# A fused attention and gating kernel: order of small steps, banks of PSUM, and where attention's two parts are added

## The chip, the cores and the metric

The kernel runs on one core of a Trainium2 chip. The metric is device time in microseconds (us) of one execution. The engines are PE (matmul, with its weight loads listed as PEld), DVE (vector), ACT (activation), POOL and SP, whose queue (SPq) issues nearly all DMA transfers. PE writes its results into PSUM, eight banks of 512 float32 values for each of 128 partitions; DVE and ACT read them there.

## The reference, cut to what matters

Two blocks follow each other on 2048 tokens of width 1024. Block A is attention with a memory, block B a gated network that mixes along the tokens.

```python
# block A: 32 heads of 32, 4 segments of 512 tokens
q, k, v = (layernorm(x) @ w for w in (wq, wk, wv))      # split into heads and segments
for s in range(4):
    p     = softmax(qs @ ks.T * scale + mask)           # inside the segment
    a_dot = p @ vs
    a_mem = (phi(qs) @ M) / (phi(qs) @ z + 1e-6)        # the memory of earlier segments
    o     = g * a_mem + (1 - g) * a_dot                 # g = sigmoid(beta), for each head
    M, z  = M + phi(ks).T @ vs, z + phi(ks).sum()
h = x + o @ wo
# block B
zz = gelu(layernorm(h) @ w_in)                          # 3584 columns
z1, z2 = zz[:, :1792], layernorm(zz[:, 1792:])
out = h + (z1 * (w_sp @ z2 + b_sp)) @ w_out
```

## The kernel before, in words

All operations are recorded in program order by `_Recorder.record`, which finds for each the earlier operations that it must wait for (by 32 bytes in SBUF and by whole banks in PSUM). `emit` then writes one instruction stream for each engine, so every engine works strictly in the order of the recording. Since `emit` issues everything at line 214, all rows of the profile have that line; they are told apart by the names of tiles.

**Attention.** The loop `for n in range(LAST + 1)` makes 32 rounds: segment `s = n // 8`, group of four heads `c = n % 8`. A round computes on PE the logits in three parts (`logits(n, 0..2)`, into banks 0 to 3), the projections of K and Q for the next round (`qk`), the product of probabilities and V for the round before (`pv(n - 1)`, into banks 4 and 5, the view `PVA`), the state update (`state`, in bank 5) and one or two tiles of other work (V projections, output projections `wo`), all of which take banks 6 and 7 in turn by `next_bank`. From segment 1 on, the third logits part is joined by `mem` (queries against the memory) and `mem_norm`, which divides it into the tile `tm` on DVE. `norm(n)` on DVE takes the reciprocal of the softmax sums (`rd`), multiplies `PVA` by it, in segment 0 straight into `otok`, otherwise into the tile `ta`, and later adds `ta` and `tm` into `otok`; between the two, `state_sum` copies the state update out of bank 5 (`msum` or `upd`), and POOL adds it to the memory. POOL also masks the exponentials (`affine_select` on `e`).

`bg_pop` advances layer norms of the next tokens by one step: apply, then reciprocal root on POOL, then statistics on DVE (`stats`). `piece_loads` and `piece_norms` load rows of the input and mixing weights of block B (`nb`) and take their absolute maximum on DVE (`sqz`, `sq`) or their squares on ACT; the table `pieces` says in which round. `scale_of(16)` in round 25 sums them with a small matmul into a bank taken by `next_bank`, and DVE reduces that bank into `tot`.

**Block B.** Products are formed in a seven-product scheme of sums of blocks. `z2_step` makes the second half of the first product; `jobs2`, filled by `at(x, f)`, hangs other work behind its steps, among it the last segment's output projection (`wo_tile`, each of its two 512-column halves being added to x on DVE as `hch`). From here on banks come from the list `free`, and how it rotates sets the later order `banks`. `z1_step` makes the first half; its weight sums `sz` are formed on POOL (`sz_sum`). `gate(pr, perm)` does the mixing over tokens for each half of the tokens, with banks given by `perm`: `perm[0:3]`, `perm[3:5]` and `perm[5:7]` in three roles. Its products are named by the mixing weights' sums, `t1` to `t4` and `b11` to `b22`; for the second half these sums are made on DVE by `q_sum`. In it ACT copies partial results (`copy_u`, tile `tmp_u`), DVE forms the gated result `z1x`, and `jobs` hangs other work behind each step, among it the squares `y0_norm` on ACT and `scale_w`. The output product at the end uses banks 0 to 6 by number.

Of the kernel before, what the change touches and what calls it, by code (L numbers as in the profile page):

```python
# [262 lines left out]
def bass_sequential_preLN__memory_aug_infini_attn__mixer_gmlp__prompt_kernel(  # L263
# [401 lines left out]
    def norm(n):  # L665
        s, c = divmod(n, NQ)
        ot = OTOK[s % 2][:, :, c * 128:(c + 1) * 128].rearrange("p q (i d) -> p q i d", d=32)
        dve.reciprocal(RD[:], PVA[:, :, :, 32])
        dve.tensor_tensor(RD[:], RD[:], OMG[:, c:c + 1, :].to_broadcast([128, 4, 4]), ALU.mult)
        rb = RD[:].unsqueeze(3).to_broadcast([128, 4, 4, 32])  # L670
        if s == 0:
            dve.tensor_tensor(ot, PVA[:, :, :, 0:32], rb, ALU.mult)
        else:
            dve.tensor_tensor(TA[:], PVA[:, :, :, 0:32], rb, ALU.mult)
        if n:
            state_sum(n)
        if n == 1:
            state_sum(0)
        if s > 0:
            dve.tensor_tensor(ot, TA[:], TM[n % 2][:], ALU.add)  # L680
        if c == NQ - 1:
            for tcl in range(4):
                to_T(OT, tcl, OTOK[s % 2][:, tcl, :])
# [238 lines left out]
    def sz(g, k):  # L922
        return SZ[k - 1 + (k == 4 and g % 2)][:]

    def sz_sum(g, k):
        fc = FC[g]
        a, b, op = {1: (wz_blk(1, 0, fc), wz_blk(1, 1, fc), ALU.add), 2: (sz(g, 1), wz_blk(0, 0, fc), ALU.subtract),
                    3: (wz_blk(0, 0, fc), wz_blk(1, 0, fc), ALU.subtract),
                    4: (wz_blk(0, 1, fc), sz(g, 2), ALU.subtract)}[k]
        pool.tensor_tensor(sz(g, k), a, b, op)  # L930

    def w_half(c, eng=dve):
        if eng is act:
# [36 lines left out]
                              apply_absolute_value=True)  # L970

    pieces = {}
    for i, (n, k, q) in enumerate(((6, 0, dve), (6, 1, dve), (7, 0, dve), (7, 1, dve), (8, 0, dve), (14, 1, dve),
                                   (15, 0, dve), (15, 1, dve), (16, 0, dve), (17, 1, dve), (10, 0, act), (11, 1, act),
                                   (12, 0, act), (13, 1, act), (18, 2, act), (19, 3, act))):
        pieces.setdefault(n, []).append((NB[k], SQZ, i, q))
# [15 lines left out]
    for n in range(LAST + 1):  # L992
        s, c = divmod(n, NQ)
        f1, f2, f3, f4 = [], [], [], []
        if n < LAST:
            f1, f2 = [("qk", n + 1, 1)], [("qk", n + 1, 0)]
        if s == 0:
            f3 = [("v", 0, c, 1)] if c < 4 else [("v", 1, c - 4, 0)]
        elif s < NSEG - 1:
            if c < 2:  # L1000
                f3, f4 = [("v", s, 2 * c, 1)], [("v", s, 2 * c + 1, 1)]
            elif c < 6:
                f3, f4 = [("wo", s - 1, c - 2, 0)], [("wo", s - 1, c - 2, 1)]
            else:
                f3, f4 = [("v", s + 1, 2 * (c - 6), 0)], [("v", s + 1, 2 * (c - 6) + 1, 0)]
        elif c < 2:
            f3, f4 = [("v", s, 2 * c, 1)], [("v", s, 2 * c + 1, 1)]
        elif c < 6:
            f3, f4 = [("wo", s - 1, c - 2, 0)], [("wo", s - 1, c - 2, 1)]
        elif c == 6:  # L1010
            f3, f4 = [("z2", 2, 0, 0)], [("z2", 2, 4, 1)]
        else:
            f1, f2 = [("z2", 2, 1, 2)], [("z2", 2, 5, 3)]
            f3, f4 = [("z2", 0, 0)], [("z2", 0, 4)]

        def fill(lst):
            for u in lst:
                {"v": proj_v, "wo": wo, "qk": proj_qk, "z2": z2_group, "qmm": q_part, "qout": qk_out,
                 "vmm": v_part, "vout": v_out}[u[0]](*u[1:])

        if s < NSEG - 1 and 0 <= c - 2 * (s == 0) < 4:
            t = c - 2 * (s == 0)
            ln_tasks(XCH[t], XNT[(s + 1) % 2], t)
        if s < NSEG - 2 and c >= 4:
            x_load(4 * (s + 2) + c - 4)
        if s > 0 and c == 1:
            xr_load(4 * (s - 1))

        if n == 0:
            fill([("vmm", 0, 3, 0, 7, 0, 5)])  # L1030
            f1 = [("vmm", 0, 3, 0, 7, 5, 8), ("vout", 0, 3, 0, 7)] + f1
            f2 = [("qmm", 1, 7, 0, 8), ("qout", 1, 0, 7), ("vmm", 0, 0, 1, 6, 0, 2)]
            f3 = [("vmm", 0, 0, 1, 6, 2, 8), ("vout", 0, 0, 1, 6)]
        piece_loads(n + 1, act)
        logits(n, 0)
        fill(f1)
        if n > 0:
            pv(n - 1, range(3))
        logits(n, 1)
        if n > 0:  # L1040
            pv(n - 1, (3,))
        if n != 2:
            bg_pop()
        fill(f2)
        if n == 2:
            bg_pop()
        logits(n, 2)
        if n < LAST:
            phi_exp(n + 1)
        piece_norms(n, act)  # L1050
        if n == 0:
            gates()
            mask_g()
        while n == LAST and staged:
            z2_gelu(*staged.pop(0))
        fill(f3)
        if n < LAST:
            phi_max(n + 1)
        bg_pop()
        fill(f4)  # L1060
        bg_pop()
        if n == 25:
            scale_of(16)
        piece_norms(n, dve)
        piece_loads(n + 1, dve)
        if n == 0:
            rot["n"] = 1
        if n == 1:
            sp.dma_start(WO[:], wcols(A_wo, 0, D))
        if n in (24, 26):  # L1070
            win_load(n - 24)
        if n == 24:
            pool.memset(ONES[:], 1.0)
            pool.memset(MHZ[:], -0.5)
            scale_in(SQZ, 10, 1.0)
        if n == 26:
            scale_end(1)
            w_half(0)
        if n == 28:
            w_half(2)  # L1080
        if n == 29:
            w_sum(0, 3, WS[0, 0])
            w_sum(0, 2, WS[0, 0])
        if n == 30:
            w_sum(0, 4, WS[0, 0])
            hn_sum(0, 1, 0)
            hn_sum(0, 1, 1)
            xr_load(4 * (NSEG - 1))
            win_load(1)
            win_load(3)  # L1090
        if n == LAST:
            hn_sum(0, 2, 0)
            hn_sum(0, 2, 1)
            hn_sum(0, 3, 0)
            hn_sum(0, 3, 1)
            w_sum(0, 1)
            hn_sum(0, 4, 0)
            hn_sum(0, 4, 1)
# [49 lines left out]
    def at(x, f, *a):  # L1148
        jobs2.setdefault(x, []).append((f, a))

    def wo_tile(tcl):
        for half in range(2):
            wo(NSEG - 1, tcl, half)
            wide.add(free[-1])
            bg_pop()

    def sj_load(i):
        r, h = 14 + i // 2, i % 2
# [14 lines left out]
    at(8, w_sum, 1, 2, WS[0, 1])  # L1173
    at(12, w_sum, 1, 1)
    for i in range(4):
        at(8 + 2 * i, wo_tile, i)
    for i in range(4):
        at(34 + 8 * i, sj_load, i)
        at(44 + 8 * i, sj_norm, i)
# [216 lines left out]
    def z1_step(g, k):  # L1396
# [18 lines left out]
        if k == 1:  # L1415
            if zb[g, 1] not in full:
                pe.matmul(PS[:, zb[g, 1], 448:512], IDENT[:], IDENT[:, 0:64], start=False, stop=False,
                          skip_group_check=True)
            act.activation(bank(zb[g, 1]), b, ACTF.Copy)
        elif k == 6:  # L1420
            dve.tensor_copy(u2, b)
        elif k == 5:
            act.activation(u3, b, ACTF.Copy)
            if g < 13:
                for x in (1, 2):
                    sz_sum(g + 1, x)
        elif k == 7:
            dve.tensor_tensor(u3, b, u3, ALU.add)
            late.append(lambda: z1_out(fc + 7, 2 * p + 1, u3))
            if g < 13:  # L1430
                sz_sum(g + 1, 3)
        elif k == 2:
            z1_out(fc, 2 * p, b)
            if g == 0:
                sz_sum(1, 4)
        elif k == 4:
            z1_out(fc + 7, 2 * p, b)
        else:
            dve.tensor_tensor(u2, b, u2, ALU.add)
            late.append(lambda: z1_out(fc, 2 * p + 1, u2))  # L1440
            if g < 12:
                sz_sum(g + 2, 4)
# [186 lines left out]
    q_sum("t2")  # L1629
    s_sum(3, 0)  # L1630
    q_sum("t3")

    OBG = {"b12": 0, "b22": 2, "t1": 1, "t2": 3, "t3": 4, "t4": 5}
    OBW = {"b11": 0, "b21": 1}
# [65 lines left out]
        jobs.setdefault((g, k), []).append((f, a))  # L1700

    for r in range(14):
        job(r // 7, (r % 7) // 2, y0_norm, r)
    for h in range(4):
        job(2 + (h + 1) // 4, (h + 1) % 4, y0_conv, h)
        job(3 + (h + 1) // 4, (h + 1) % 4, y_sum, h + 1, 0)
    job(2, 0, y0_scale)
    job(0, 0, q_sum, "t4")
    job(0, 0, scale_w)
    for r in range(7):  # L1710
        job(1, 0, ob_load, "b12", r)
# [14 lines left out]
        for f, a in jobs.get((g, k), ()):  # L1726
            f(*a)

    gate(1, [banks[k] for k in (0, 3, 5, 1, 2, 4, 6)], each=each1)

    def o_prod(b, a, w, first, lo=0, hi=512):
        for i in range(7):
# [3 lines left out]
    def iv(g):  # L1736
        return (INVO0 if g < 3 else INVO)[:]

    def o_p1(g):
        o_prod(g % 3, y_blk(0, 0, g), "b11", True)  # L1740
        act.activation(OT4[g % 2][0][:], bank(g % 3), ACTF.Copy, scale=iv(g))

    def o_adds(g, ks=(1, 2, 3)):
        for k in ks:
# [4 lines left out]
        dve.scalar_tensor_tensor(o, PS[:, b, lo:hi], iv(g), add, ALU.mult, ALU.add)  # L1749

    def o_p2(g):
        o_prod(g % 3, y_blk(0, 1, g), "b21", False)

    def o_c11(g):
        f = FIN2[g % 4][:, 0, 0, :]
        o_stt(g, f, g % 3, f)
        fin_out(g, 0, 0)

    fin_in(2)
# [2 lines left out]
    o_adds(0)  # L1762
    ob_sum("t4", 3)
    for g in range(NG):
        bb, bc = 3 + g % 2, 5 + g % 2
        end = g == NG - 1
        last = ((bc, 0, 512),) if not end else ((bc, 0, 384), (7, 384, 512))
        f1, f12, f22, f21 = OT4[g % 2]
# [65 lines left out]
```

## Time and profile before

| what | value |
|---|---|
| median of 3 runs | 744.46 us (743.98 to 744.66) |
| the profiled execution's own time | 744.07 us |
| its span in the profile | 742.4 us |
| PE busy | 730.3 us (98%) |
| DVE busy | 582.3 us (78%) |
| ACT busy | 478.6 us (64%) |
| POOL busy | 276.4 us (37%) |
| granted PE clock | 1.0 throughout |

The profile shows one execution. Times in the timeline count from the start of the span: attention runs to about 310 us, the second half of block B's first product to about 396, its first half to about 483, the mixing of the first half of the tokens to 568, of the second half from 582 to about 655, the output product to the end. In a timeline row the first number is the start, the second the duration of the merged run, then come the engine, the operation, the tiles (out<-in), the shape and how many instructions were merged; a bracket gives the engine's idle time before the row and what ended it. Matmul records of 512 columns last 0.38 us, though one starts every 0.22 us, because they are pipelined; single matmul records can be missing.

### The profile page before, as it was taken

To read this page: it belongs to the slowest core of one execution; us is meant where nothing else is said; L and a number is where in the kernel's file an instruction comes from. 1 tells how busy PE (TensorE), PEld (TensorE's weight loads), DVE (VectorE), ACT (ScalarE), POOL (GpSimd) and SP (SyncE) were. 2 spreads that over 40 slices of the span, in tenths; PEclk is the share of its full clock that TensorE was granted. 3 is DMA by queue.
4 is the path that set the end of the run, shared out by engine and by line. 5 is a ranking of instruction groups with operands and counts; after the bars stand their busy time and mean duration, and the time that the engine had idled before them with its cause. 6 is when DMAs were issued, how large, how long until landed. Compare 5 with 4: busy or idle time off the path is not lost.

```text
span 742.4 us, 13475 instructions
## 1 busy us (share of the span) xinstructions
PE 730.3 (98%) x5333; PEld 351.7 (47%) x5399; DVE 582.3 (78%) x1026; ACT 478.6 (64%) x684; POOL 276.4 (37%) x424
## 2 busy tenths in 40 slices
PE   8999999999999999999999999999999999999998
PEld 4444445445555445545554444444444444444444
DVE  5577889889988989878896767875556688866676
ACT  6777889888887888826886669966866283210000
POOL 2565455555654343110054899600000100005342
PEclk9999999999999999999999999999999999999999
DMA  9655668457635852645050036399539211031311
GB/s 302 173 171 125 136 145 178 130 147 167 172 100 158 255 178 58 171 125 132 29 141 1 1 57 129 54 202 183 173 119 320 81 41 35 1 114 64 107 57 57
DMA packets 148798, 92.64 MB, mean 125 GB/s; under 512 B 105984, under 2 KB 132864, under 8 KB 148224
## 3 DMA queue, kind: packets, MB, share of 16 engines
q1 hardware_dynamic: 147920, 91.00, 47.0%
q8 instruction: 42, 0.69, 0.4%
q10 hardware_dynamic: 816, 0.79, 0.3%
q14 instruction: 20, 0.16, 0.1%
HBM read 56.11 MB, written 12.58 MB: 93 GB/s over the span
## 4 chain that ended last, share of the span: by engine, by line
PE 87%; DVE 8%; ACT 2%; issue 1%; DMA 1%; POOL 0%; DVEq 0%
PE ps L214 87%; DVE stats L214 2%; DVE sqz L214 1%; DMA wv<-in_A_wv_dram 1%; DVE hch L214 1%; DVE otok L214 1%; DVE pqk L214 1%; ACT e L214 1%; DVE ta L214 0%; DVE rd L214 0%; DVE rdm L214 0%; DVE etmp L214 0%; POOL sz L214 0%; DVE tm L214 0%; DVE sq L214 0%
## 5 line engine op out<-in xcount | busy, mean ns | idle before, releaser
L214 ACT ACTIVATE e<-ps 128x2048 bf16<-128x2048 f32 (+1 forms) x96 | 152.7, 1591 | 21.3 <-PE ps L214 20.6
L214 POOL TENSOR_SCALAR_AFFINE_SELECT e<-e 128x512 bf16<-128x512 bf16 x128 | 91.2, 726 | 123.1 <-ACT e L214 122.9
L214 PE MATMUL ps<-xnT,wk 128*128 128x512 bf16 x233 | 59.6, 380 | 1.8 <-ACT v L214 0.4
L214 PE MATMUL ps<-wv,xnT 128*128 128x512 bf16 x255 | 59.3, 380 | 1.4 <-DMA wv<-in_A_wv_dram 1.0
L214 POOL TENSOR_TENSOR ot<-ot,fin 128x512 f32<-128x512 f32 x21 | 27.8, 1351 | 86.5 <-ACT ot L214 86.5
L214 PE MATMUL ps<-wo,oT 128*128 128x512 bf16 x254 | 57.9, 380 | 0.9 <-DVE hch L214 0.8
L214 PE MATMUL ps<-xnT,wq 128*128 128x512 bf16 x226 | 54.0, 379 | 1.6
L214 PEld LDWEIGHTS ps<-v,e 128*128 128x128 bf16 x1280 | 38.8, 96 | 14.0 <-issue 6.5
L214 ACT ACTIVATE ot<-ps,invo 128x512 f32<-128x512 f32 x7 | 4.8, 688 | 60.8 <-PE ps L214 60.8
L214 PE MATMUL ps<-v,e 128*128 128x33 bf16 x1280 | 42.2, 178 | 0.0
L214 POOL TENSOR_TENSOR sz<-wzh 128x512 f16<-128x512 f16 x28 | 34.0, 1217 | 11.2 <-PE ps L214 11.1
L214 DVE BATCH_NORM_STATS2 zst<-z 128x6 f32<-128x448 bf16 x64 | 38.1, 611 | 0.0
L214 ACT ACTIVATE tmp_u<-ps,invy 128x512 f32<-128x512 f32 x14 | 9.6, 686 | 44.2 <-PE ps L214 44.2
L214 PEld LDWEIGHTS ps<-wo,oT 128*128 128x128 bf16 x256 | 24.0, 98 | 28.6 <-DVE hch L214 1.3
L214 PE MATMUL ps<-z2h,sy 128*128 128x512 f16 (+2 forms) x182 | 37.4, 363 | 0.0
L214 PEld LDWEIGHTS ps<-xnT,wk 128*128 128x128 bf16 x256 | 22.6, 98 | 30.6 <-issue 4.5
L214 ACT ACTIVATE qk<-ps 128x512 bf16<-128x512 f32 x48 | 28.8, 600 | 12.9 <-PE ps L214 12.9
L214 PEld LDWEIGHTS ps<-wv,xnT 128*128 128x128 bf16 x256 | 23.2, 98 | 27.9 <-DMA wv<-in_A_wv_dram 1.2
L214 DVE TENSOR_TENSOR zt<-ps,zt 128x512 f32<-128x512 f32 x28 | 19.1, 686 | 22.1 <-PE ps L214 17.6
L214 PE MATMUL ps<-qk 32*128 32x128 bf16 (+3 forms) x512 | 34.5, 302 | 0.7 <-DVE tm L214 0.5
L214 PEld LDWEIGHTS ps<-xnT,wq 128*128 128x128 bf16 x256 | 23.5, 97 | 22.9 <-issue 0.2
L214 ACT ACTIVATE ps<-ps 128x512 f32<-128x512 f32 (+1 forms) x42 | 23.9, 568 | 14.0 <-PE ps L214 14.0
(280 smaller groups left out, 1673.3 us busy)
## 6 DMA issues: line engine op xcount, KB each, us to landing
nb<-in_B_w_in_dram SPq DMA_DIRECT2D x16, 448.0 KB, 4.0
nb<-in_B_w_sp_dram SPq DMA_DIRECT2D x14, 512.0 KB, 4.7
w_out<-in_B_w_out_dram SPq DMA_DIRECT2D x6, 896.0 KB, 5.3
xch<-in_A_x_dram SPq DMA_DIRECT2D x16, 256.0 KB, 4.3
xr<-in_A_x_dram SPq DMA_DIRECT2D x16, 256.0 KB, 3.9
out_dram<-hch SPq DMA_DIRECT2D x16, 256.0 KB, 2.4
w_spT<-stg SPq DMA_DIRECT2D x16, 256.0 KB, 4.1
out_dram<-fin SPq DMA_DIRECT2D x31, 128.0 KB, 1.7
```

What stands on the lines that cost most here:

```text
L214: ins = getattr(e, op.name)(*op.args, **op.kw)
```

## The change

It does this:

- In `norm`, segments 1 to 3 write the product of `PVA` and `rd` back into `PVA` in PSUM instead of into `ta`, and the sum with `tm` follows at once, ahead of `state_sum`'s copy.
- The absolute maximum with index 4 moves from round 8 to round 5, and its load from the end of round 7 to the end of round 4.
- In round 8 the first `bg_pop` comes after `logits(n, 2)`.
- After `scale_of(16)` the rotation of banks 6 and 7 goes on by one.
- The first output projection of the last segment is split: its second half comes one `z2_step` later.
- One weight sum, `sz_sum(1, 2)`, runs on DVE instead of POOL.
- The sum `t4` is made before the second `gate` instead of behind its first step, and the squares `y0_norm` start one step later, two for each step.
- The output product takes its banks from the second `gate`'s order (`obank`) instead of by number.

```diff
@@ norm(n)
-            dve.tensor_tensor(TA[:], PVA[:, :, :, 0:32], rb, ALU.mult)
+            dve.tensor_tensor(PVA[:, :, :, 0:32], PVA[:, :, :, 0:32], rb, ALU.mult)
+        if s > 0:
+            dve.tensor_tensor(ot, PVA[:, :, :, 0:32], TM[n % 2][:], ALU.add)
         if n:
             state_sum(n)
         if n == 1:
             state_sum(0)
-        if s > 0:
-            dve.tensor_tensor(ot, TA[:], TM[n % 2][:], ALU.add)
@@ sz_sum
-    def sz_sum(g, k):
+    def sz_sum(g, k, eng=pool):
...
-        pool.tensor_tensor(sz(g, k), a, b, op)
+        eng.tensor_tensor(sz(g, k), a, b, op)
@@ pieces
-    for i, (n, k, q) in enumerate(((6, 0, dve), (6, 1, dve), (7, 0, dve), (7, 1, dve), (8, 0, dve), (14, 1, dve),
+    for i, (n, k, q) in enumerate(((6, 0, dve), (6, 1, dve), (7, 0, dve), (7, 1, dve), (5, 0, dve), (14, 1, dve),
@@ the loop over rounds
-        if n != 2:
+        if n not in (2, NQ):
             bg_pop()
         fill(f2)
         if n == 2:
             bg_pop()
         logits(n, 2)
+        if n == NQ:
+            bg_pop()
...
         if n == 25:
             scale_of(16)
+            rot["n"] += 1
@@ the last segment's output projection
-    def wo_tile(tcl):
-        for half in range(2):
-            wo(NSEG - 1, tcl, half)
-            wide.add(free[-1])
-            bg_pop()
+    def wo_half(tcl, half):
+        wo(NSEG - 1, tcl, half)
+        wide.add(free[-1])
+        bg_pop()
...
-        at(8 + 2 * i, wo_tile, i)
+        at(8 + 2 * i, wo_half, i, 0)
+        at(8 + 2 * i + (i == 0), wo_half, i, 1)
@@ z1_step, k == 5
-                    sz_sum(g + 1, x)
+                    sz_sum(g + 1, x, dve if (g, x) == (0, 2) else pool)
@@ before the second gate
     q_sum("t3")
+    q_sum("t4")
@@ jobs of the second gate
     for r in range(14):
-        job(r // 7, (r % 7) // 2, y0_norm, r)
+        job(*divmod(1 + r // 2, 4), y0_norm, r)
...
-    job(0, 0, q_sum, "t4")
     job(0, 0, scale_w)
...
-    gate(1, [banks[k] for k in (0, 3, 5, 1, 2, 4, 6)], each=each1)
+    perm1 = [banks[k] for k in (0, 3, 5, 1, 2, 4, 6)]
+    gate(1, perm1, each=each1)
@@ output product
+    obank = [perm1[k] for k in (1, 2, 0, 4, 3, 6, 5)]
...
-        o_prod(g % 3, y_blk(0, 0, g), "b11", True)
-        act.activation(OT4[g % 2][0][:], bank(g % 3), ACTF.Copy, scale=iv(g))
+        o_prod(obank[g % 3], y_blk(0, 0, g), "b11", True)
+        act.activation(OT4[g % 2][0][:], bank(obank[g % 3]), ACTF.Copy, scale=iv(g))
...
-        bb, bc = 3 + g % 2, 5 + g % 2
+        bb, bc = obank[3 + g % 2], obank[5 + g % 2]
```

More of the change, by code (lines that the diff above doesn't have):

```diff
@@ L1751, in o_p2 @@
     def o_p2(g):
-        o_prod(g % 3, y_blk(0, 1, g), "b21", False)
+        o_prod(obank[g % 3], y_blk(0, 1, g), "b21", False)
     def o_c11(g):
         f = FIN2[g % 4][:, 0, 0, :]
-        o_stt(g, f, g % 3, f)
+        o_stt(g, f, obank[g % 3], f)
         fin_out(g, 0, 0)
```

## The prediction

> **What bounds the kernel now.** I read the page's busy times first, then the list of waits for PE, then the stretches of the timeline around each of those waits.
>
> ```profile
> PE 730.3 (98%) x5333; PEld 351.7 (47%) x5399; DVE 582.3 (78%) x1026; ACT 478.6 (64%) x684; POOL 276.4 (37%) x424
> ```
>
> PE is busy for 730.3 of 742.4 us, and no other engine is near that. The matmuls stay, so only PE's 12 us of idle time can be won, and part of those lie before the first matmul and behind the last. The list of waits names the others:
>
> ```profile
> PE ps L214 <- DVE hch L214: 1.0, 2, 0.8
> PE ps L214 <- DVE tm L214: 0.5, 1, 0.5
> PE ps L214 <- ACT tmp_u L214: 0.5, 1, 0.5
> PE ps L214 <- ACT v L214: 0.4, 1, 0.4
> ...
> PE ps L214 <- POOL sz L214: 0.3, 1, 0.3
> ```
>
> The columns are the total, the count and the longest. These are single events, and the change touches each of them. Here is each in the timeline, with what PE waited for:
>
> ```profile
> 85.33 3.63 PE L214 MATMUL ps<-wv,xnT 128*128 128x512 bf16 x16
> ...
> 86.70 1.41 DVE L214 BATCH_NORM_STATS2 stats<-xch 128x6 f32<-128x512 bf16 x2
> ...
> 88.72 0.69 DVE L214 TENSOR_TENSOR tm<-ps,rdm 128x512 f32<-128x512 f32 x1
> ...
> 89.47 0.39 PE L214 MATMUL ps<-qk 32*128 32x512 bf16 x4 [0.51 <-DVE tm L214]
> ...
> 249.78 0.17 DVE L214 TENSOR_REDUCE tot<-ps 128x1 f32<-128x16 f32 x1 [0.31 <-PE ps L214]
> ...
> 250.39 1.90 PE L214 MATMUL ps<-xnT,wk 128*128 128x512 bf16 x7 [0.35 <-ACT v L214]
> ...
> 318.00 1.90 PE L214 MATMUL ps<-wo,oT 128*128 128x512 bf16 x8 [0.78 <-DVE hch L214]
> ...
> 400.48 1.45 POOL L214 TENSOR_TENSOR sz<-wzh 128x512 f16<-128x512 f16 x1 [6.86 <-PE ps L214]
> ...
> 403.31 1.89 PE L214 MATMUL ps<-z1x,sz 128*128 128x512 f16 x8 [0.29 <-POOL sz L214]
> ...
> 594.48 1.90 PE L214 MATMUL ps<-t4g,z2h 128*128 128x512 f16 x8 [0.49 <-ACT tmp_u L214]
> ```
>
> The first row gives the rate: sixteen matmuls in 3.63 us, the last recorded for 0.38, so one starts every 0.217 us. The record of the last before a gap thus overhangs by 0.16 us, and a bracket understates what PE lost by about that.
>
> **Part by part.**
>
> *Statistics after the memory normalisation (round 8).* `bg_pop` now stands behind `logits(8, 2)`, so the two statistics (1.41 us) and their aggregate (0.21) follow `tm` instead of delaying it. Rounds 8, 9, 10 and 11 begin at 79.40, 89.47, 98.89 and 108.31: round 8 lasts 10.07 us where its followers last 9.42, and the difference of 0.65 is the prize. Afterwards `tm` ends near 87.9, 0.9 before PE wants its bank. This pop issues only statistics: no DMA, nothing on POOL.
>
> *One absolute maximum from round 8 to round 5.* Its 2.01 us on DVE now come at about 66.3 and push K's copy for round 7 from 66.45 to 68.3. That bank is wanted by V at 69.96, and `etmp` waits for ACT until 71.65 anyway. Q's copy ends near 70.9, and its reader starts at 71.79: 0.9 of cover. Its 448 KB load moves with it from SP's queue at the end of round 7, where it stood ahead of attention's transposes, to the end of round 4, ahead of an x load. The next load into that buffer must now wait for the maximum, until 68.3, where SP was free at 67.95: 0.3 us later, and its reader starts at 72.64 against 4.0 us to land. I put it at nothing; if the cover fails, the whole 0.3 to 0.9 goes on the path.
>
> *Banks after `scale_of(16)` (round 25).* K's first matmul comes 0.74 us after the logits there, against 0.33 in the rounds before and after (240.45 to 240.78, 259.25 to 259.58): 0.41 is lost to V's evacuation. K now takes the bank that `tot` reads. That reduce ends at 249.95, and DVE hands over in 0.06 (`tm` to 89.47), so K starts at 250.01 instead of 249.98. Gain 0.38.
>
> *Attention's sum from PSUM, 24 rounds.* These groups carry the price:
>
> ```profile
> L214 DVE TENSOR_TENSOR otok<-ta,tm 128x512 bf16<-128x512 f32 x24 | 22.3, 930 | 0.3
> ...
> L214 DVE TENSOR_TENSOR zt<-ps,zt 128x512 f32<-128x512 f32 x28 | 19.1, 686 | 22.1 <-PE ps L214 17.6 <-ACT z1T L214 4.4
> ...
> L214 DVE TENSOR_TENSOR ta<-ps,rd 128x512 f32<-128x512 f32 x24 | 16.6, 691 | 0.8
> ```
>
> The sum reads `ta` and `tm` from SBUF and takes 930 ns in the mean, 691 at best and over 1,000 beside POOL's selects. With one operand in PSUM its nearest row is `zt`, 686. The product keeps its inputs but writes PSUM in place; no DVE instruction of this trace writes there. ACT does, in 568 ns (`ps<-ps`) against 600 into SBUF (`qk<-ps`), so I take 691 for the product, with 0.6 below and twice the streaming time, 1.22, above, if reading and writing one bank took turns. The pair falls from 1.62 to 1.38 us, DVE loses 24 x 0.24 = 5.8 us, and nearly none of it is on the path. Two waits stand on this chain: 0.11 at 165.05, where the old sum took 0.86, and 0.31 near 269, where it already took 0.69. The first gives 0.05, the second nothing. Behind the sum, the state copy and POOL's update come up to 0.7 later; the banks are wanted again 5 us on.
>
> [...]
>
> *Halves of the last projection.* The second half waits for the first one's sum, since it takes the same bank. Lost: 0.78 + 0.16 = 0.94. Four 448-column matmuls (319.73 to 320.49, 0.76) now go in between and only change places. The rest, 0.18, stays. Gain 0.76.
>
> *One weight sum to DVE.* PE lost 0.29 + 0.16 = 0.45. POOL's first sum ends at 401.93, and its second fills 402.01 to 403.16. DVE's sum, 0.42 (`z2h<-z2h`, 512 f16), is done by 402.5; PE wants it at 402.86. DVE stands until then with `wzh` (0.74) queued behind, so that ends near 403.2; next comes `zt` at 403.12, which delays only its own activation. Gain 0.45.
>
> *Norms and `t4`.* `tmp_u` (593.75 to 594.42) was late because ACT ran two squares (0.84 and a read of 0.19 each) first. Without them it follows its matmuls, at 592.3 to 593.0, and PE wants the bank at 593.82. `t4` (2.29) moves in front of `z1x`, where DVE was idle for 4.67. ACT then runs six squares of 0.95, not five, before `tmp_u` of the next group: 593.0 to 598.7, where that can start at 599.2. Six follow in the next group instead of five, so the last ends near 611.4 instead of 610.4, still ahead of the next `tmp_u` (611.95) and of PE's sum of them (615.21). Gain 0.49 + 0.16 = 0.65.
>
> *Output banks.* They follow the new order of banks so that each first use falls on one long free. PE shows no gap at that seam, so zero; without this, about 0.75 (a `z1x` row).
>
> **Sum:** 0.65 + 0.38 + 0.05 + 0.76 + 0.45 + 0.65 = 2.94 us. The profiled execution took 744.07, so 741.13; the median of the runs, 744.46, lies 0.39 higher and would give 741.52. I take the middle, 741.3.
>
> **Rivals.**
>
> 1. *Part of it becomes other waits.* What is late next is close in two places: `tot` at 249.95 against 249.98, DVE's weight sum 0.4 ahead. If these two pay nothing, the gain is 2.1 and the time 742.2. For it: the margins; against: the rest have 0.8 or more. 0.14.
> 2. *The write into PSUM costs 1.22.* The pair is then 1.91. At 165.05 it grows from 0.69 + 0.86 = 1.55, so 0.36 comes back; near 269 DVE runs without a pause through two rounds whose pairs grow from 1.38, so 1.06. Rounds with `hch` or an absolute maximum behind the pair may add another 0.2 to 1. That leaves a gain of 0.5 to 1.3, 743.2 to 744, within 0.2%. ACT's row speaks against. 0.07.
> 3. *Slower: both operations at 1.22.* The pair of 2.45 is 0.83 longer than the mean now. An ordinary round has 0.41 of slack (`tm` ends at 98.42 and hands over in 0.06, PE starts at 98.89), so each of the 16 rounds of segments 1 and 2 pays 0.42, 6.7 in all; less 2.94 that ends near 748. It decides from a pair of about 2.2, where 16 x 0.18 eats the gain. Nothing in the rows speaks for it but that the form is new. 0.05.
> 4. *The change does not do what it says:* the new order of banks puts a wait where there was none. Each step above finds its bank read 0.1 us or more before it is wanted, except where said. A whole new wait of 0.8 to 1.5 us leaves 742.1 to 742.8. 0.05.
>
> **Chances and range.** The forecast gets 0.69. A measurement here cannot tell less than 0.2%, or 1.5 us, from no change. Faster holds the forecast, the first rival and most of the fourth: 0.87. Same 0.07, slower 0.06. The range goes from 740.7 (the runs' spread of 0.35 each way and all of the projection's wait) to 742.5 with rival 1: about 0.8.
>
> **What would show it.** In the changed profile PE's list should have lost `tm`, `tmp_u`, `sz` and `v`, with `hch` down to 0.2 or 0.4 and the 0.3 near 268 still there. `otok<-ps,tm` should stand near 690 and `ps<-ps,rd` near 690. A `ps<-ps,rd` over 0.95, a PE wait on `tm` in many rounds, or one on `qk` near 71 would prove me wrong.

## The result, and the profile after

| what | before | after |
|---|---|---|
| median of 6 runs each, taken together | 744.22 us (743.43 to 745.21) | 741.11 us (740.89 to 741.8) |
| the profiled execution's own time | 744.07 us | 741.11 us |
| its span | 742.4 us | 739.5 us |
| first round-3 logits to last matmul (below) | 697.98 us | 695.42 us |

The ratio of the times is 0.996, with a 95% interval of 0.9947 to 0.9972: faster by 0.3 to 0.5%. The forecast was 741.3. It was nearly met, but not by its own sum: one of its gains was given back, and scatter in the first microseconds of the execution filled part of the hole.

That scatter matters for all that follows. The programs of all these runs are nearly the same in the first 13 us, and yet these move by up to 2.1 us between executions. The traces with a granted clock of 1.00 throughout reach round 3 between 40.91 and 41.66 us. Two traces with a lower clock at the start come later: in that of the first experiment (e1) it was 0.87 between 5 and 10 us and 0.79 between 10 and 15, with round 3 at 43.19; in that of the last kernel (best_max_27) it was 0.73 and 0.93 (0.998 over the whole execution in both), with round 3 at 42.45. A single time can therefore not settle a term of 0.4 us. So I also compare a **stretch** of each trace: from the 512-column logits matmuls of round 3 (at 41.33 us before, 41.05 after) to the start of the last matmul, worked out from the recorded starts. Two traces of the kernel after give 695.42 and 695.45. Of the kernel before there is one trace.

First the line of PE, and PE's list of waits (total, count, longest) of the kernel after.

```profile
PE 733.4 (99%) x5399; PEld 351.7 (48%) x5399; DVE 579.5 (78%) x1027; ACT 478.0 (65%) x684; POOL 267.0 (36%) x423
```

```profile
PE ps L214 <- DVE etmp L214: 1.2, 1, 1.2
PE ps L214 <- DVE tm L214: 0.6, 1, 0.6
PE ps L214 <- DMA wv<-in_A_wv_dram: 0.6, 1, 0.6
PE ps L214 <- DVE xnT L214: 0.3, 1, 0.3
PE ps L214 <- DVE hch L214: 0.2, 1, 0.2
```

PE's busy time went up only in the records: all 5399 matmuls stand here, where the page before had 5333. The list says more. `tmp_u`, `sz` and `v` are gone, and so is the 0.8 of `hch`. `tm` is not: it stands at 0.6, and this is not the old event. `etmp`, `wv` and `xnT` belong to the start of the program. Next, the timeline of the kernel after around the seven places (start, duration, engine, operation, tiles, count, idle before and its releaser):

```profile
86.89 0.69 DVE L214 TENSOR_TENSOR tm<-ps,rdm 128x512 f32<-128x512 f32 x1
...
87.50 1.41 DVE L214 BATCH_NORM_STATS2 stats<-xch 128x6 f32<-128x512 bf16 x2
...
88.59 0.40 PE L214 MATMUL ps<-qk 32*128 32x512 bf16 x4
...
164.00 0.40 PE L214 MATMUL ps<-qk 32*128 32x512 bf16 x4
...
248.73 0.17 DVE L214 TENSOR_REDUCE tot<-ps 128x1 f32<-128x16 f32 x1 [0.31 <-PE ps L214]
...
248.96 1.90 PE L214 MATMUL ps<-xnT,wk 128*128 128x512 bf16 x8
...
267.67 0.39 PE L214 MATMUL ps<-qk 32*128 32x512 bf16 x4 [0.59 <-DVE tm L214]
268.26 1.90 PE L214 MATMUL ps<-xnT,wk 128*128 128x512 bf16 x8 [0.20 <-DVE hch L214]
...
317.04 1.90 PE L214 MATMUL ps<-wo,oT 128*128 128x512 bf16 x8
...
399.95 0.42 DVE L214 TENSOR_TENSOR sz<-sz,wzh 128x512 f16<-128x512 f16 x1 [1.40 <-POOL sz L214]
400.27 2.75 PE L214 MATMUL ps<-z1x,sz 128*128 128x512 f16 x12
...
591.64 1.89 PE L214 MATMUL ps<-t4g,z2h 128*128 128x512 f16 x8
```

The five waits of PE that the forecast shows with a bracket have none any more; the logits at 267.67 have a new one. These are the first ones of round 28, and they wait for `tm` of round 27. Matching the PE instructions of the two traces one by one gives what each place moved (minus: the kernel after comes earlier by so much more):

| place (us in the kernel after) | step, us | forecast |
|---|---|---|
| start, first 13 us | -0.29 | nothing |
| end of round 8, 88.59 | -0.58 | -0.65 |
| logits of round 17, 164.00 | -0.18 | -0.05 |
| K after `scale_of(16)`, 248.96 | -0.39 | -0.38 |
| logits of round 28, 267.67 | **+0.48** | nothing |
| second half of the projection, 317.04 | -0.76 | -0.76 |
| weight sum, within the row at 400.27 | -0.46 | -0.45 |
| `t4`, 591.64 | -0.66 | -0.65 |

Without the start the steps add up to -2.55, and the stretches differ by 2.56 (697.98 - 695.42); the forecast's sum was -2.94. With the start the steps come to -2.84, as the spans do.

The operations in the new form, from the groups by line and shape (count | busy time, mean ns | idle before); the third line is POOL's:

```profile
L214 DVE TENSOR_TENSOR ps<-ps,rd 128x512 f32<-128x512 f32 x24 | 16.8, 699 | 0.8
L214 DVE TENSOR_TENSOR otok<-ps,tm 128x512 bf16<-128x512 f32 x24 | 16.6, 692 | 0.8
L214 POOL TENSOR_SCALAR_AFFINE_SELECT e<-e 128x512 bf16<-128x512 bf16 x128 | 83.9, 669 | 127.1 <-ACT e L214 127.1
```

The product written into PSUM in place takes 699 ns, the sum 692, a pair of 1.39 us where 1.38 was forecast. The two rivals that needed 1.22 for one or both of them fall. The 1.22 was an estimate, and the rows of the kernel before bear it: DVE's copies from PSUM take 284 ns there for 132 float32 columns (`upd`) and 673 for 512 (`zt`), so 512 columns more would cost some 524, and 691 + 524 is 1.215 us.

**Where the 0.48 went.** Between `tot` and `tm`, DVE runs through two rounds of work. These are rows of the timeline of DVE in the kernel before:

```profile
249.78 0.17 DVE L214 TENSOR_REDUCE tot<-ps 128x1 f32<-128x16 f32 x1 [0.31 <-PE ps L214]
...
254.85 0.18 DVE L214 TENSOR_TENSOR rd<-rd,omg 128x16 f32<-128x16 f32 x1
...
257.03 0.17 DVE L214 TENSOR_SCALAR rdm<-ps 128x16 f32<-128x16 f32 x1 [0.55 <-ACT e L214]
...
264.36 1.13 DVE L214 TENSOR_SCALAR wih<-win,sc 128x3584 f16<-128x3584 bf16 x1
```

In the same trace POOL's masks start behind `rd` and `wih`:

```profile
255.21 2.49 POOL L214 TENSOR_SCALAR_AFFINE_SELECT e<-e 128x512 bf16<-128x512 bf16 x3 [2.40 <-ACT e L214]
...
264.40 2.18 POOL L214 TENSOR_SCALAR_AFFINE_SELECT e<-e 128x512 bf16<-128x512 bf16 x2 [2.12 <-ACT e L214]
```

And these are DVE and POOL in the kernel after:

```profile
253.78 1.22 POOL L214 TENSOR_SCALAR_AFFINE_SELECT e<-e 128x512 bf16<-128x512 bf16 x2 [2.01 <-ACT e L214]
253.80 0.63 DVE L214 TENSOR_TENSOR rd<-rd,omg 128x16 f32<-128x16 f32 x1
...
255.81 0.16 DVE L214 TENSOR_SCALAR rdm<-ps 128x16 f32<-128x16 f32 x1
...
262.96 2.07 POOL L214 TENSOR_SCALAR_AFFINE_SELECT e<-e 128x512 bf16<-128x512 bf16 x2 [2.12 <-ACT e L214]
263.13 1.41 DVE L214 TENSOR_SCALAR wih<-win,sc 128x3584 f16<-128x3584 bf16 x1
...
266.92 0.69 DVE L214 TENSOR_TENSOR tm<-ps,rdm 128x512 f32<-128x512 f32 x1
```

`tot` starts on the small matmul of `scale_of(16)`, which stands ahead of K. The rotation moves K, not `tot`, so it doesn't move DVE's run. From the start of `tot` to the hand-over of `tm`, 0.06 before the logits, DVE takes 18.78 us before (249.78 to 268.56) and 18.88 after (248.73 to 267.61). Before, 0.55 of that was idle, since `rdm` had to wait for its round; with the hand-over this pause cost 0.63 (the sum starts 1.24 before `rdm` there, 0.61 after). With PE 0.39 earlier, 0.24 of it should have stayed. But the masks on POOL came earlier too, one now 0.02 ahead of `rd` and one 0.17 ahead of `wih`. From start to start, `rd` to the product grew from 0.21 to 0.67, and `wih` to the next from 1.05 to 1.33, together by 0.74. That is the whole pause and 0.11 more, against 0.10 in the run. So nothing of the 0.39 reached round 28, and 0.09 was lost on top.

The rows show how long the two operations stood beside the masks. The first of the two masks runs for about 0.61 (half of 1.22), from 253.78 to 254.39, and `rd` ends at 254.43, 0.63 after its start; in the kernel before, where it was done before the mask began, it took 0.18. With the same 0.61 for the second mask, `wih` stood 0.44 beside it and took 0.28 longer (1.41 against 1.13), where `rd` stood 0.59 beside its mask and took 0.45 longer: each pays some 0.15 less than the overlap. How a mask slows an operation of DVE is not shown by these runs. The group of masks points the same way: 726 ns in the mean before, 669 after. Of all the edits, that of `norm` makes this difference; whether by the sum's operand in PSUM or by its new place, no run tells. The first row is of the kernel before with only that edit (e3 below), the second of the kernel after without it (e4):

```profile
L214 POOL TENSOR_SCALAR_AFFINE_SELECT e<-e 128x512 bf16<-128x512 bf16 x128 | 83.3, 664 | 130.3 <-ACT e L214 130.2
```

```profile
L214 POOL TENSOR_SCALAR_AFFINE_SELECT e<-e 128x512 bf16<-128x512 bf16 x128 | 91.1, 725 | 121.2 <-ACT e L214 121.1
```

### The profile page after: what moved, and what is told of

Its sections match the earlier page's. It is cut to its first block, busy times and chain, and to the rows that moved or that the text cites. A ratio compares the mean times of both kernels' runs of the same rounds, so it can differ in the third digit from the quotient of the medians.

```text
span 739.5 us, 13541 instructions
## 1 busy us (share of the span) xinstructions
PE 733.4 (99%) x5399; PEld 351.7 (48%) x5399; DVE 579.5 (78%) x1027; ACT 478.0 (65%) x684; POOL 267.0 (36%) x423
## 4 chain that ended last, share of the span: by engine, by line
PE 96%; DVE 3%; DMA 1%; issue 0%; ACT 0%; DVEq 0%
PE ps L214 96%; DVE sq L214 1%; DMA wv<-in_A_wv_dram 1%; DVE hch L214 0%; DVE ps L214 0%; DVE otok L214 0%; DVE rd L214 0%; DVE wih L214 0%; DVE stats L214 0%; ACT L214 0%; DVE rdm L214 0%; DVE pqk L214 0%; DVE fin L214 0%; DVEq L224 0%; DVE tot L214 0%
## 5 line engine op out<-in xcount | busy, mean ns | idle before, releaser
L214 POOL TENSOR_SCALAR_AFFINE_SELECT e<-e 128x512 bf16<-128x512 bf16 x128 | 83.9, 669 | 127.1 <-ACT e L214 127.1
L214 PE MATMUL ps<-xnT,wq 128*128 128x512 bf16 x256 | 60.5, 379 | 0.0
```

What stands on the lines that cost most here:

```text
L214: ins = getattr(e, op.name)(*op.args, **op.kw)
```

## The experiments

Each is the kernel after with one edit, unless it says otherwise. Most were run once, so their times carry the start's scatter, and the stretch decides. All stretches, in us:

| kernel | stretch | against after (695.42) | time of its run |
|---|---|---|---|
| before | 697.98 | +2.56 | 744.07 |
| e3_psum_alone (on before) | 697.78 | +2.36 | 743.57 |
| e5_by_number | 696.47 | +1.05 | 742.12 |
| e7_t4_only | 696.10 | +0.68 | 741.61 |
| e6_squares_only | 696.09 | +0.67 | 742.04 |
| e4_sbuf_sum | 695.60 | +0.18 | 741.88 |
| e8_max_back | 695.58 | +0.16 | 741.63 |
| e1_no_skip | 695.34 | -0.08 | 743.15 |
| e9_27_no_skip | 694.90 | -0.52 | 741.04 |
| e2_max_27 | 694.49 | -0.93 | 740.58 |

### e1_no_skip: without the rotation

```diff
             scale_of(16)
-            rot["n"] += 1
```

> The changed kernel without the extra step of the bank rotation after scale_of(16). In the changed kernel K's first matmul of round 26 came 0.39 us sooner than before (its lead grew from 1.05 to 1.44 us), but at the next logits, 267.67, the lead was down to 0.96 and PE waited 0.59 for DVE's tm. Theory A: from tot (248.73) to tm (267.61) DVE runs without a pause, so it alone sets the start of those logits, and the gain of the rotation is given back there. Then K of round 26 waits 0.35 again for ACT's v, but the logits at 267.67 start within 0.1 of where they do now, PE's wait for tm falls to 0.2 to 0.3, and the time at the end is within 0.15 of the changed kernel. Theory B: the wait on tm is a chance of this one execution, the rotation's gain lasts: then everything from 249 on comes 0.35 to 0.4 later than in the changed kernel.

Measured: the wait for V's evacuation is back, and the one on `tm` is gone. Two rows of its timeline:

```profile
251.49 1.90 PE L214 MATMUL ps<-xnT,wk 128*128 128x512 bf16 x8 [0.35 <-ACT v L214]
...
269.73 0.39 PE L214 MATMUL ps<-qk 32*128 32x512 bf16 x4
```

PE loses 0.39 at K and gains 0.48 at the logits of round 28; the stretch is 0.08 shorter than with the rotation. The time, 743.15, is no evidence: 2.1 of it lie in the first 13 us, at the lower clock told of above. In this kernel the mask starts behind `rd`, which takes 0.17 again; `wih` takes 1.14, and DVE is idle for 0.54 ahead of `rdm`, as before:

```profile
255.95 0.17 DVE L214 TENSOR_TENSOR rd<-rd,omg 128x16 f32<-128x16 f32 x1
...
256.31 1.22 POOL L214 TENSOR_SCALAR_AFFINE_SELECT e<-e 128x512 bf16<-128x512 bf16 x2 [2.40 <-ACT e L214]
...
258.13 0.17 DVE L214 TENSOR_SCALAR rdm<-ps 128x16 f32<-128x16 f32 x1 [0.54 <-ACT e L214]
```

So the rotation as it stands in the changed kernel is worth nothing, which was the first theory.

### e2_max_27: more room on DVE

If DVE's run sets the logits of round 28, taking work out of it must bring the 0.48 back. One absolute maximum (2.2 us) goes from round 26 to round 27.

```diff
-                                   (25, 6, dve), (26, 6, dve), (20, 2, act), ...
+                                   (25, 6, dve), (27, 6, dve), (20, 2, act), ...
```

> The changed kernel with one absolute maximum (2.2 us on DVE, the last of the eight on the mixing weights) moved from the end of round 26 to the end of round 27. Theory A (DVE's unbroken run from tot to tm sets the logits at 267.67): without these 2.2 us in the run tm ends about 2 us sooner, both waits at 267.67 (0.59) and 268.26 (0.20) go, and all that follows comes 0.7 to 1.1 us sooner: 740.0 to 740.4 by the profiled execution where the changed kernel took 741.11. Theory B (something else, such as the handover between the engines, sets those logits): the two waits stay and the time stays within 0.2. A rival to the profit under A: the 2.2 us come back as a wait on DVE in round 28 or 29, near 277 to 295.

Measured: both waits are gone, and no new one came in rounds 28 and 29. PE's whole list of waits, and the logits of round 28:

```profile
PE ps L214 <- DVE etmp L214: 1.2, 1, 1.2
PE ps L214 <- DMA wv<-in_A_wv_dram: 0.8, 1, 0.8
PE ps L214 <- DVE lno L214: 0.2, 1, 0.2
```

```profile
267.41 0.39 PE L214 MATMUL ps<-qk 32*128 32x512 bf16 x4
267.73 1.90 PE L214 MATMUL ps<-xnT,wk 128*128 128x512 bf16 x8
```

What is left belongs to the start. The stretch is 0.93 shorter than the changed kernel's. That is more than the 0.48 that was given back: what the kernel before had lost here goes as well: 0.18 at the logits (3.74 after the sixteen matmuls' start, where 3.56 is the rule) and 0.26 at K (0.59 after the logits, where 0.33 is). 0.48 + 0.18 + 0.26 is 0.92. In this kernel `rd` still takes 0.63 (at 254.21), and `wih` 1.13 (at 261.35); the longer `rd` costs nothing, since DVE is idle for 0.86 later in the run:

```profile
265.18 0.17 DVE L214 TENSOR_SCALAR rdm<-ps 128x16 f32<-128x16 f32 x1 [0.86 <-ACT e L214]
```

### e9_27_no_skip: the same room, without the rotation

```diff
-                                   (25, 6, dve), (26, 6, dve), (20, 2, act), ...
+                                   (25, 6, dve), (27, 6, dve), (20, 2, act), ...
@@
             scale_of(16)
-            rot["n"] += 1
```

> The last but one kernel (maximum in round 27) without the step of the bank rotation after scale_of(16). Theory A (the rotation is worth 0.39 us, and was given back only because DVE's unbroken run set the logits at 267): now that DVE has room there, leaving the step out costs 0.35 to 0.4 from 249 on, and PE waits again 0.35 for ACT's v. Theory B (the rotation is worth nothing in itself): no lasting difference, as in the run without the step alone.

Measured: the wait on V costs 0.39 at K, and nothing is given back later; the stretch is 0.41 longer than with both edits.

```profile
249.83 1.90 PE L214 MATMUL ps<-xnT,wk 128*128 128x512 bf16 x8 [0.35 <-ACT v L214]
```

The four kernels make a square. Without room on DVE the rotation is worth -0.08; with room it is worth 0.41. The step's mechanism in the forecast was right, and so was its size; what lay behind it on DVE took it away.

### e3_psum_alone and e4_sbuf_sum: attention's sum

The first is the kernel before with only the edit of `norm`; the second is the kernel after with the old `norm`.

```diff
# e3, on the kernel before
-            dve.tensor_tensor(TA[:], PVA[:, :, :, 0:32], rb, ALU.mult)
+            dve.tensor_tensor(PVA[:, :, :, 0:32], PVA[:, :, :, 0:32], rb, ALU.mult)
+        if s > 0:
+            dve.tensor_tensor(ot, PVA[:, :, :, 0:32], TM[n % 2][:], ALU.add)
         ...
-        if s > 0:
-            dve.tensor_tensor(ot, TA[:], TM[n % 2][:], ALU.add)
```

> The kernel before with only the edit of norm: the product is written back into PSUM and the sum follows it at once. Prediction: the wait of 0.11 at 165.05 shrinks by 0.05 and nothing else moves on PE. Rival from the changed kernel's profile: the sum falls from 930 to 692 ns in all 24 rounds and the whole 0.18 at 165.05 goes. Both: the six other waits stay as they were (0.51 on tm at 89.47, 0.35 on v at 250.39, 0.78 on hch at 318, 0.29 on sz, 0.49 on tmp_u), and the time is within 0.3 of the kernel before. If the DVE time as such were worth something (24 x 0.24 = 5.7 us), it would be 2 us or more faster.

> The changed kernel with the old norm: product into ta in SBUF, state copy, then the sum of ta and tm. If the edit is worth only what the wait at 165.05 held, this is 0.05 to 0.2 us slower than the changed kernel, by a PE wait on tm near 164, and the sum is back near 930 ns. Rival: in the order of round 8 after the change tm stands right behind the longer sum, and the run of DVE up to 267 is longer too, so the edit also covers other places: then there are new waits of 0.1 to 0.5 near 268, and 0.3 to 0.8 are lost in all.

Measured: e3 gains 0.18 at the logits of round 17 and next to nothing anywhere else (0.20 over the stretch); the other waits of the kernel before stand in its list unchanged. e4 loses 0.17 at the same place and nothing after it. The rows of e4 there:

```profile
161.06 3.63 PE L214 MATMUL ps<-wv,xnT 128*128 128x512 bf16 x16
164.78 0.39 PE L214 MATMUL ps<-qk 32*128 32x512 bf16 x4
```

In e3, sixteen matmuls from 161.02 are followed by the logits at 164.58, 3.56 later; here it is 3.72. So the sum from PSUM is worth 0.17 to 0.20, all of it in one round, although it saves DVE 24 x 0.23 = 5.5 us (930 + 691 against 699 + 692 ns). The rival of e4, that the old sum brings waits near 268, is false.

### e5_by_number: the output product's banks

```diff
-    obank = [perm1[k] for k in (1, 2, 0, 4, 3, 6, 5)]
+    obank = list(range(7))
```

> The changed kernel with the output product's banks by number (0 to 6) as before, while the order of the banks of the second gate is the new one (5, 2, 3, 4, 6, 0, 1; it was 5, 2, 3, 0, 6, 4, 1). Then the first product takes bank 0, which the last step of the gate still reads. Prediction: a PE wait of about 0.75 us for DVE at the seam near 652, where the changed kernel has none. Rival: the read of bank 0 is over by the time (no wait, same time), so that the new order of banks is worth nothing by itself.

Measured: one new wait, at the seam.

```profile
662.68 0.75 DVE L214 SCALAR_TENSOR_TENSOR vb<-ps,invy,tmp_u 128x512 bf16<-128x512 f32 x1 [0.98 <-PE ps L214]
663.48 1.68 PE L214 MATMUL ps<-w_out0h,z1x 128*128 128x512 f16 x7 [0.85 <-DVE vb L214]
```

PE starts the output product 1.04 later by the step in its lead. The seam lies at 662.46 in the kernel after and at 665.30 before, some 10 us behind the place that the expectation and the overview of the stages give. The edit gains nothing against the kernel before; it is needed because the order of banks has changed ahead of it.

### e6_squares_only and e7_t4_only: the two halves of one step

```diff
# e6: t4 back behind the second gate's first step
-    q_sum("t4")
...
+    job(0, 0, q_sum, "t4")
# e7: the squares back where they were
-        job(*divmod(1 + r // 2, 4), y0_norm, r)
+        job(r // 7, (r % 7) // 2, y0_norm, r)
```

> The changed kernel with the sum t4 back behind the first step of the second gate; the squares stay one step later. The kernel before named ACT's tmp_u as what PE waited for (0.49) in front of the product with t4. Theory A, as the prediction put it: only the squares held PE up, t4 was made in time; then no wait comes back. Theory B: t4 itself ended at 594.10, where PE wanted it at 593.82, so that both were late and the list named the later; then a wait for DVE of 0.1 to 0.2 (0.3 with the overhang of the last matmul) comes back near 591.6, and perhaps some 0.2 more behind it, as vb waits behind t4 and holds a bank.

> The changed kernel with the squares back at their old steps; t4 stays in front of the gate. Both theories of the last run expect the wait for ACT's tmp_u to come back, 0.35 to 0.5 us, 0.5 to 0.65 with the overhang. If the product waited for t4 alone, it would not.

Measured: each loses 0.67 to 0.68 over the stretch, which is the whole step. The first rows are of e6, the last one of e7.

```profile
589.93 2.28 DVE L214 TENSOR_TENSOR t4g<-b21g,t2g 128x4096 f16<-128x4096 f16 x1
...
592.13 0.18 DVE L214 TENSOR_REDUCE tot<-ps 128x1 f32<-128x28 f32 x1
...
592.36 1.89 PE L214 MATMUL ps<-t4g,z2h 128*128 128x512 f16 x8 [0.26 <-DVE tot L214]
```

```profile
592.16 1.90 PE L214 MATMUL ps<-t4g,z2h 128*128 128x512 f16 x8 [0.49 <-ACT tmp_u L214]
```

The bracket of e6 names `tot`, which stands right behind `t4` on DVE and ended last. But `tot` reads bank 7, which the products of `gate` don't use; the operand that came late is `t4`, done at 592.21. Of e6's loss 0.45 lies at this product and 0.20 at the next two, the first of which waits for `vb`, also behind `t4` on DVE.

In the kernel before, two things ended late within 0.3 us of each other: `tmp_u` on ACT, which the list named, and `t4` on DVE, which it didn't:

```profile
591.81 2.29 DVE L214 TENSOR_TENSOR t4g<-b21g,t2g 128x4096 f16<-128x4096 f16 x1
...
593.75 0.67 ACT L214 ACTIVATE tmp_u<-ps,invy 128x512 f32<-128x512 f32 x1
```

With either edit alone the other one sets the start.

### e8_max_back: the absolute maximum in round 8

```diff
-    for i, (n, k, q) in enumerate((... (7, 1, dve), (5, 0, dve), ...
+    for i, (n, k, q) in enumerate((... (7, 1, dve), (8, 0, dve), ...
```

> The changed kernel with the absolute maximum of index 4 back in round 8. The prediction put the move at nothing, and the gain of 0.65 at round 8 to the later statistics alone. If so, round 8 still begins its successor 0.58 to 0.65 sooner than before, and the time is within 0.1 of the changed kernel. Rival: with the maximum behind it DVE runs late in round 9, and its tm now stops the logits of round 10: a wait of 0.1 to 0.3 us near 98.

Measured: round 8 keeps its gain, and round 9 is 0.13 longer (88.97 to 98.53, 9.56, against 88.59 to 98.02, 9.43). So the rival holds: `tm` of round 9 ends at 98.47, 0.06 ahead of those logits. Without the move, 0.13 of round 8's gain of 0.58 is given back in the next round.

### after_again and best_max_27: the version that beats both

These are the kernel after once more and e2's kernel, compared with the same runs of the kernel before.

> The changed kernel unedited, timed in the same call for comparison: 741.1 us as before, 0.4% faster than the kernel before.

> The changed kernel with one absolute maximum on the mixing weights at the end of round 27 instead of 26, timed. Its single look was 740.58 us, of which the start cost 0.4 more than in the changed kernel's profiled execution and the stretch from 267 on 0.93 less. If the 0.93 is lasting, it is 0.9 us faster than the changed kernel beside it, near 740.2, and 0.5% faster than the kernel before. If the start's scatter is all, they are equal.

| kernel | median | ratio to before, 95% interval | stretch |
|---|---|---|---|
| before | 743.58 us (10 runs) | | |
| after_again | 741.33 us (740.51 to 741.85, 6 runs) | 0.9969 (0.9957 to 0.9981) | 695.45 |
| best_max_27 | 740.53 us (739.58 to 741.64, 5 runs) | 0.9961 (0.9949 to 0.9974) | 694.50 |

By the medians the best kernel is 0.8 us ahead of the changed one; the intervals overlap, so the times alone don't prove it. The stretches differ by 0.95, and by 0.93 in the first pair.

## Why the prediction was right, and where it was not

**The total** came out at 741.11 against a forecast of 741.3, in the range. The sum behind it was 0.38 too large (2.94 against 2.56). In the profiled execution the start, 0.29 earlier by chance, hid part of this (e3, which is the kernel before up to round 8, also reached round 3 at 41.05); in the second comparison the medians differ by 2.25, in the first by 3.11, and the sum of 2.56 lies between them.

**The step that failed: "Banks after `scale_of(16)` ... Gain 0.38."** The gain came, 0.39, and 0.48 was given back 19 us later. The step asked whether the bank was free, and it was. It did not ask what is late next: `tm` of round 27 hangs on DVE, whose run starts at `tot`, and `tot` doesn't move with K. The forecast knew the place. It put 0.31 of waiting near 269 at "the second nothing", since the sum took 0.69 there already, and it said in the second rival that "DVE runs without a pause through two rounds". That reading was wrong by one row: DVE had a pause of 0.55, and a pause is room that an earlier PE uses up. Rival 1 held that the rotation could pay nothing, but for a margin of 0.03 at `tot`, which was not the cause. e1, e2 and e9 show that DVE's work between `tot` and `tm` decides. That the masks on POOL ate the rest of the room is read from the rows above and from the way they change in e1; no run moved a mask alone.

**Statistics in round 8, 0.65:** 0.58 came. That is the whole wait: from the sixteen matmuls to the logits it was 4.14 us before and is 3.55 now. The forecast took the difference of whole rounds, but round 8 still lasts 9.48 us where its followers last 9.42, without any wait in it. **The absolute maximum, "at nothing":** its arrival in round 5 cost nothing, as said, but its departure from round 8 was worth 0.13. The step weighed only what it cost where it went, not what it freed where it left.

**Attention's sum, 0.05:** 0.17 to 0.20. The price was right (699 and 692 ns against 691 and 686), though the ACT row taken as support does not bear on it: 568 is a mean of two shapes (585 for 512 columns, 534 for 448), and these copies read one bank and write another, so they say nothing of a product in place. The size was wrong. By the step's own numbers the pair falls from 1.55 to 1.38 there, by 0.17, which covers the bracket of 0.11 and more; it gives 0.05 without a working. Nor did it add anything for the overhang here, as it did with the other brackets; it is 0.07 at this place (3.74 us from the sixteen matmuls to the logits, where 3.56 is the rule, and a bracket of 0.11). The runs show all of the 0.17. The sum with a PSUM source is at 692 in the mean where the best with two SBUF sources was 691, so in this shape the source made a difference of 1 ns.

**Halves 0.76 and weight sum 0.45:** 0.76 and 0.46, as worked out. The row at 400.27 runs through twelve matmuls without a gap, and DVE's sum in front of it took 0.42.

**`t4` and the squares, 0.65:** 0.66, but not for the reason given. The prediction put the wait on ACT's squares alone and took the move of `t4` into idle time as a thing beside it. e6 shows that without the move nothing is gained.

**Output banks, "without this, about 0.75":** the need was right, the size was 1.04. The reader that holds the bank is a `vb`, not a `z1x`, and it starts 0.98 after DVE fell idle.

**What it said one would see:** PE's list lost `tmp_u`, `sz` and `v`. It did not lose `tm`, and `hch` at 0.2 is not the rest of the projection's wait but the old second event, at 269.21 before and 268.26 now. None of its three signs of being wrong appeared.

## What to carry to other kernels

When an edit brings PE forward, ask at the next places where PE meets the engine that was close behind whether that engine comes forward too; if its run starts at an event that the edit doesn't move, the gain lasts only as long as the pauses in that run. A list of waits names the one that came last: look up when every other operand was ready before costing a fix, because two things late within 0.3 us of each other can need two edits, and here each alone was worth nothing. Where terms are of 0.4 us and the start scatters by more, compare a stretch between two fixed instructions rather than the whole time.

## What the runs showed of the hardware that was not expected

A DVE product that reads and writes the same PSUM bank in place takes 699 ns for 128x512 float32, 8 more than into SBUF. The edit of `norm`, by which the sum takes one of its two operands from PSUM, brought POOL's masks from 726 to 664 ns in the mean (e3), and the sum went from 930 to 692 (kernel after). A DVE operation that took 0.18 us ahead of a POOL mask in the kernel before took 0.63 in the kernel after, where the mask started 0.02 us before it, and one of 1.13 took 1.41 with the mask 0.17 ahead of it: a shift of some tenths on a third engine, which is what the edit made, changes which of two operations comes first. And the clock granted to PE is not constant over a profiled execution whose mean is 0.998: in one of them (e1) it was 0.87 between 5 and 10 us and 0.79 between 10 and 15, and that execution reached round 3 2.1 us after the kernel after (43.19 against 41.05). In another (best_max_27) it was 0.73 and then 0.93, and that one came there 1.0 later than the other trace of the same kernel (42.45 against 41.45).
